# An mLSTM cell and a GELU layer: the layer's float32 block products replaced by three float32r products of 12-bit parts

## The chip, the cores and the metric

The kernel runs on one core of a Trainium2 chip. The metric is the device time of one execution in microseconds (us): 517.14 us is the median of three executions of the kernel before (516.58 to 518.07). The profile shows one execution, of 515.2 us from its first to its last instruction. PE is the matrix engine, PEld its weight loads, DVE the vector engine, ACT the scalar (activation) engine, POOL the general engine, SP the queue that issues most transfers.

## The reference, cut to what matters

```python
B, H, S, D = 4, 8, 768, 40          # q, k, v, o_gate: (B,H,S,D); i_gate, f_gate: (B,H,S)
for t in range(S):                   # the mLSTM cell, stabilised by a running maximum m
    m_new = maximum(f[t] + m, i[t])
    C = exp(f[t] + m - m_new) * C + exp(i[t] - m_new) * outer(v[t], k[t])
    n = exp(f[t] + m - m_new) * n + exp(i[t] - m_new) * k[t]
    y[t] = sigmoid(o[t]) * (C @ q[t]) / maximum(abs(n @ q[t]), 1)
    m = m_new
x = y as (3072 tokens, 320)
h = x @ w_in                         # (320, 2048)
out = (0.5 * h * (1 + erf(h / sqrt(2)))) @ w_out      # (2048, 320)
```

The weights arrive as float64; both kernels fetch their bits and convert them to float32 on chip. The sequence is cut into six chunks of 128 time steps. A chunk holds 512 tokens (four batches of 128 steps). Chunk 0 is handled in a front part, together with the conversion of the weights; "later chunks" are chunks 1 to 5. "The cell" of a chunk is its share of the mLSTM; "up" is `x @ w_in` and "down" is `gelu(h) @ w_out`.

## The kernel before: the parts that matter here

The later chunks compute up and down in float32 with a block scheme in which 7 products of half-size blocks take the place of 8 (sums of blocks of the weights, of x and of the hidden values are formed by DVE). Up works on two 128-row blocks of x (`NX = 2`), plus a rest of 64 rows that is done directly, with two halves side by side in the array.

```python
def product(to, lhs, rhs, f0, first, last):            # up: one block product, 2 tiles, moving 256 columns
    for j in range(2):
        nc.tensor.matmul(to[:, j, :], lhs[:, (f0 + j) * P:(f0 + j + 1) * P], rhs, ...)      # L597

def products(f0, to_sum):                              # seven of them for each pair of 128-wide tiles
    c11, c12, c21, c22 = [pool.tile([P, 2, HT], F32, name="pu", tag=tag)
                          for pool, tag in ((ps_tr, "tr"), (ps_h, "h"), (ps_mm, "a"), (ps_mm, "b"))]
    product(c11, a11, b11, f0, True, False)
    nc.scalar.copy(out=blk[1][1], in_=c11)
    product(c12, s2, t2, f0, True, True)
    nc.vector.tensor_tensor(out=blk[0][0], in0=c12, in1=blk[1][1], op=OP.add)
    ...                                                # c21, c22, then c11, c12, c21 again

def rest(f0, pair, h):
    for j in range(2):
        for e in range(2):
            nc.tensor.matmul(pair[e][:, j, :], w_rest[halves[e], ...], xT[halves[e], NX, ...], ...)   # L626
...
add_to = lambda blk, e, h, x, y: (
    nc.vector.tensor_tensor(out=blk[e][h], in0=x, in1=y, op=OP.add),                        # L639
    nc.scalar.activation(out=blk[e][h], in_=blk[e][h], func=AF.Gelu))                       # L640

# down: seven products, each in two steps t of 8 matmuls with 160 moving columns (HD = 160)
for j in range(HF):
    nc.tensor.matmul(bank[at][:, i, :], lhs(j, t), rhs(j), ...)                             # L682
return [lambda ...: product(...) for x in todo for t in range(2)]       # 14 steps, "F" in the order below

# a later chunk: all of up, then down interleaved with the cell of the next chunk
DOWN = """M0 Z M1 T0 W0 F F T1 W1 Z G3 Z F S0 Z S1 C0 M2 Z C1 G1 G0 M3 V0 Y0 Z V1 W2 Z F F T2 W3 F T3 F G2 Z
    Y1 S2 S3 C2 V2 C3 Y2 V3 F F Y3 X0 F F X1 X2 F F X3 F"""
```

The letters are steps of the next chunk's cell for batch 0 to 3: M masks on POOL, T transposes q and k (two PSUM banks, copied out by ACT), W eight exponentials on ACT, G a sigmoid on ACT, S scores (two banks, multiplied with W by DVE), C carries the state (one bank, read by three DVE operations), V values (one bank), Y the division on DVE and POOL, X transposes y to x (one bank). The banks for T and X come from a pool of two (`ps_tr`); S, C and V also use `ps_mm` and `ps_h`.

Of the kernel before, what the change touches and what calls it, by code (L numbers as in the profile page):

```python
# [9 lines left out]
F32 = mybir.dt.float32  # L10
BF16 = mybir.dt.bfloat16
# [6 lines left out]
I23 = 2.0 ** 23  # L18

# [8 lines left out]
    K K J T0 W0 O6 M2 O7 A J W1 S0 C0 K J T1 L7 U U K Z K V0 T2 A M3 J J G1 S1 K W2 W3 K C1 Z A S2 Z V1 G2 J Y0 J K  # L28
    C2 Z T3 J K Y1 U U J S3 Z V2 C3 K J K K J J F K F F F Z J K J X0 K K J F F F Z J F K G3 Y2 F J K V3 J K F K X1 J
    J F F F F K Z X2 B8 J F Y3 X3 B9 F"""  # L30
DOWN = """
    M0 Z M1 T0 W0 F F T1 W1 Z G3 Z F S0 Z S1 C0 M2 Z C1 G1 G0 M3 V0 Y0 Z V1 W2 Z F F T2 W3 F T3 F G2 Z Y1 S2 S3 C2
    V2 C3 Y2 V3 F F Y3 X0 F F X1 X2 F F X3 F"""
# [3 lines left out]
def kernel(  # L37
# [41 lines left out]
    outp = ctx.enter_context(tc.tile_pool(name="outp", bufs=2))  # L79
# [8 lines left out]

    w_in = const.tile([P, NX, 2, DFF // 2], F32, name="w_in")
    w_rest = const.tile([P, DFF // 2], F32, name="w_rest")
    w_out = const.tile([P, NF, DM], F32, name="w_out")
# [3 lines left out]
    xT = const.tile([P, NX + 1, TG], F32, name="xT")  # L98
# [31 lines left out]
    def load_M(n):  # L130

        if n >= NCH * B:
            return
        c, b = divmod(n, B)
        Mb[n] = wts.tile([P, H, L], F32, name="Mb", tag="Mb", bufs=NM)
        nc.sync.dma_start(out=Mb[n].rearrange("p h l -> p (h l)"),
                      in_=M_d[c - 1, b * H:(b + 1) * H, :].rearrange("h l -> (h l)").unsqueeze(0).to_broadcast([P, H * L]))
# [113 lines left out]
    for f in range(0, DFF // 2, WP // 2):  # L251
        for x in range(NX):
            pieces.append(([w_src["in"][x * P:(x + 1) * P, w_cols(e, f, WP // 2)] for e in range(2)],
                           w_in[:, x, :, f:f + WP // 2]))
        if f % WP == 0:
            pieces.append(([w_src["in"][NX * P:DM, w_cols(e, f, WP)] for e in range(2)], w_rest[:, f:f + WP]))
    n_in = len(pieces)
    for f in range(NF):
        pieces.append(([w_src["out"][f * P:(f + 1) * P, :]], w_out[:, f, :]))
# [32 lines left out]
    def conv_two(i):  # L292

        if i < len(pieces):
            hi, p = bits.pop(i)[:, :, 1], pow2.pop(i)
            pu = p.bitcast(U32)
            nc.vector.scalar_tensor_tensor(out=pu, in0=hi, scalar=0x80000000, in1=pu,
                                           op0=OP.bitwise_and, op1=OP.bitwise_or)
            dst, s = pieces[i][1], sig.pop(i)
            if len(dst.shape) == 3:  # L300
                s, p = [t.rearrange("p (e f) -> p e f", e=2) for t in (s, p)]
            nc.vector.scalar_tensor_tensor(out=dst, in0=s, scalar=2.0 ** -20, in1=p, op0=OP.mult, op1=OP.mult)
            fetch(i + NB)
# [18 lines left out]
    class Cell:  # L322
# [14 lines left out]
        def weights(self, b):  # L337

            n = self.c * B + b
            W[n] = wts.tile([P, H, L], F32, name="W", tag="W")  # L340
            if self.c > 0:
                M_n = Mb.pop(n)
# [37 lines left out]
        def weigh_values(self, b):  # L380
            vw = self.vw[b] = two.tile([P, H, D1], F32, name="vw", tag="vw")
# [3 lines left out]
        def scores(self, b):  # L385
# [3 lines left out]
            pool, tag = (ps_tr, "tr") if self.c > 0 and b % 2 else (ps_mm, "a")  # L389
# [10 lines left out]
        def carry(self, b):  # L400
# [4 lines left out]
            pf = ps_h.tile([P, H + NP, D1], F32, name="pf", tag="h")  # L405
# [10 lines left out]
            if c > 0:  # L416
# [4 lines left out]
                self.far[b] = two.tile([P, H, D1], F32, name="far", tag="far")  # L421
# [13 lines left out]
        def values(self, b):  # L435
# [3 lines left out]
            pool, tag = (ps_mm, "a") if self.c > 1 else (ps_h, "h")  # L439
# [9 lines left out]
            nc.vector.tensor_tensor(out=hs, in0=ph, in1=self.far.pop(b), op=OP.add)  # L449

# [11 lines left out]
        def turn_y(self, b):  # L462
# [8 lines left out]
            nc.scalar.copy(out=xT[:, :, t], in_=px)  # L471
            if self.c > 0:
                load(n + NLD)
            if self.c > 0 and b == B - 1:
                sum_x()


    HF, HT, HD = NF // 2, TG // 2, DM // 2

    Bm = [[lambda j, e=e, n=n: w_out[:, HF * e + j, HD * n:HD * (n + 1)] for n in range(2)] for e in range(2)]
    w_sums, in_sums, x_sums = [], [], []
    T = {1: lambda j: w_sums[0][:, j, :], 2: lambda j: w_sums[1][:, j, :], 3: Bm[0][1]}

    def sums_begin():

        gate_ctx.close()
        pool = ctx.enter_context(tc.tile_pool(name="sums_of", bufs=1))
        w_sums.extend(pool.tile([P, HF, HD], F32, name=f"w_sums{n}") for n in range(2))
        in_sums.extend(pool.tile([P, DFF // 2], F32, name=f"in_sums{n}") for n in range(3))
        x_sums.extend(pool.tile([P, HT], F32, name=f"x_sums{n}") for n in range(3))

    def weight_sum(n):
        x, y = {1: (Bm[0][1], Bm[0][0]), 2: (Bm[1][1], T[1]), 3: (Bm[1][1], Bm[0][1])}.get(n) or (Bm[1][0], T[2])  # L500
        if n == 4:

            parts = [raw.tile([P, 3, HD], F32, name="t4", tag=tag) for tag in ("sig", "pow", "sig")]
            T[4] = lambda j: parts[j // 3][:, j % 3, :]

        def step(j):
            nc.vector.tensor_tensor(out=T[n](j), in0=x(j), in1=y(j), op=OP.subtract)

        return [lambda j=j: (step(j), step(j + 1)) for j in range(0, HF, 2)]

    class Hidden:


        def __init__(self, summed):
            self.t = gp.tile([P, NF, TG], F32, name="g", tag="g")
            if summed:
                self.s1, self.s2 = [[raw.tile([P, HF // 2, HT], F32, name="sums", tag="bits", bufs=NB)
                                     for _ in range(2)] for _ in range(2)]

    def hidden_sums(g, f0, f1):  # L520

        (a11, a21), (_, a22) = [[g.t[:, HF * e + f0:HF * e + f1, HT * h:HT * (h + 1)] for h in range(2)]
                                for e in range(2)]
        s1, s2 = [t[f0 // (HF // 2)][:, f0 % (HF // 2):f0 % (HF // 2) + f1 - f0, :] for t in (g.s1, g.s2)]
        nc.vector.tensor_tensor(out=s1, in0=a21, in1=a22, op=OP.add)
        nc.vector.tensor_tensor(out=s2, in0=s1, in1=a11, op=OP.subtract)
        nc.vector.tensor_tensor(out=a21, in0=a11, in1=a21, op=OP.subtract)

    def up_step(g, sets):

        banks = []
        for k, (i0, i1, t0, t1) in sets:
            banks.append([ps_mm.tile([P, i1 - i0, t1 - t0], F32, name="pu", tag="ab"[k % 2]) for e in range(2)])
            for e in range(2):

                for i in range(i0, i1):
                    for x in range(NX):
                        nc.tensor.matmul(banks[-1][e][:, i - i0, :], w_in[:, x, e, i * P:(i + 1) * P], xT[:, x, t0:t1],  # L538
                                         start=(x == 0 and i == i0), stop=False, skip_group_check=True)
        for pu, (_, (i0, i1, t0, t1)) in zip(banks, sets):  # L540
            for i in range(i0, i1):
                for e in range(2):
                    r = halves[e]
                    nc.tensor.matmul(pu[e][:, i - i0, :], w_rest[r, i * P:(i + 1) * P], xT[r, NX, t0:t1], start=False,  # L544
                                     stop=(i + 1 == i1), skip_group_check=True)
        for pu, (_, (i0, i1, t0, t1)) in zip(banks, sets):
            for e in range(2):
                nc.scalar.activation(out=g.t[:, i0 + HF * e:i1 + HF * e, t0:t1], in_=pu[e], func=AF.Gelu)
# [12 lines left out]
    def first_up():  # L561
        if len(ups) == 1:
            tags_next.append(1)
        if ups:
            up_step(first_g, ups)
# [6 lines left out]
    def in_sum(i):  # L572
        f, (a11, a12), (a21, a22) = slice(WP * (i // 4), WP * (i // 4 + 1)), *[[w_in[:, x, e, :] for x in range(NX)]
                                                                               for e in range(2)]
        s1, s2, s4 = in_sums
        to, x, y, op = ((s1, a21, a22, OP.add), (s2, s1, a11, OP.subtract), (a21, a11, a21, OP.subtract),
                        (s4, a12, s2, OP.subtract))[i % 4]
        nc.vector.tensor_tensor(out=to[:, f], in0=x[:, f], in1=y[:, f], op=op)

    def x_blocks():  # L580
        return [[xT[:, x, HT * h:HT * (h + 1)] for h in range(2)] for x in range(NX)]

    def sum_x():
        (b11, b12), (b21, b22) = x_blocks()
        t1, t2, t4 = x_sums
        for to, x, y in ((t1, b12, b11), (t2, b22, t1), (b12, b22, b12), (t4, b21, t2)):
            nc.vector.tensor_tensor(out=to, in0=x, in1=y, op=OP.subtract)

    def summed_up(g, sums_too):
        (a11, s3), (a12, a22) = [[w_in[:, x, e, :] for e in range(2)] for x in range(NX)]  # L590
        s1, s2, s4 = in_sums
        (b11, t3), (b21, b22) = x_blocks()
        t1, t2, t4 = x_sums
        def product(to, lhs, rhs, f0, first, last):

            for j in range(2):
                nc.tensor.matmul(to[:, j, :], lhs[:, (f0 + j) * P:(f0 + j + 1) * P], rhs, start=(first and j == 0),  # L597
                                 stop=(last and j == 1), skip_group_check=True)

        def products(f0, to_sum):  # L600

            blk = [[g.t[:, HF * e + f0:HF * e + f0 + 2, HT * h:HT * (h + 1)] for h in range(2)] for e in range(2)]
# [196 lines left out]
```

## Time and profile before, and how to read them

| part of the 515.2 us | from, to (us) | length |
|---|---|---|
| front: chunk 0, gates, conversion of the weights, cell of chunk 1 | 0 to 133.19 | 133.2 |
| each of chunks 1 to 3: up, then down with the next chunk's cell | 133.19, 212.77, 292.35 | 79.6 each |
| chunk 4 | 371.93 | 77.7 |
| chunk 5 (no cell left) | 449.64 | 65.6 |

| engine | busy us | share of the span |
|---|---|---|
| PE | 500.3 | 97% |
| DVE | 340.2 | 66% |
| ACT | 255.0 | 49% |
| POOL | 60.9 | 12% |

Matmuls are pipelined, so the mean duration that a row prints is longer than the distance from one to the next. What a stream of matmuls costs is read from the chain of waits, which prints the length of a run of them together with their count. A float32 matmul of the source appears as two matmul records.

### The profile page before, as it was taken

The page shows a single profiled execution, that of the slowest core. Times are in us where ns is not written, and L with a number is a line of the kernel's source. Part 1 is how long each engine was busy: PE and PEld are TensorE (multiplying, and loading weights), DVE is VectorE, ACT ScalarE, POOL GpSimd, SP SyncE. Part 2 cuts the span into 40 slices and gives each one's busy share as a digit, 9 for nine tenths or more (in the row PEclk, how much of TensorE's full clock was granted, in tenths as well). Part 3 has the DMA queues.
Part 4 walks back from the last instruction along what each step waited for, and adds up shares of the span by engine and source line. Part 5 has one row for each costly group of instructions (what it writes and reads, how often), then busy time and mean ns, then how long its engine had stood idle before and what let it go on. Part 6 is the DMA issues. An engine that isn't in the chain of part 4 may idle for free.

```text
span 515.2 us, 10957 instructions
## 1 busy us (share of the span) xinstructions
PE 500.3 (97%) x4472; PEld 450.6 (87%) x4472; DVE 340.2 (66%) x696; ACT 255.0 (49%) x523; POOL 60.9 (12%) x98
## 2 busy tenths in 40 slices
PE   4889999999999999999999999999999999999997
PEld 3778888767888999988999988999988999988997
DVE  7789598999577887347668347678347657237621
ACT  7696999555344960152980132982123882124300
POOL 3002100000210225000145000053000021000000
PEclk9799999999999999999999999999999999999999
DMA  6999751279900254900234900124920020000001
GB/s 128 223 214 212 184 147 53 64 163 171 198 0 1 84 116 58 167 0 2 74 88 69 167 28 1 43 83 81 166 52 2 5 80 1 27 27 0 1 2 51
DMA packets 111442, 41.62 MB, mean 81 GB/s; under 512 B 101184, under 2 KB 104416, under 8 KB 111392
## 3 DMA queue, kind: packets, MB, share of 16 engines
q1 hardware_dynamic: 111392, 40.92, 37.5%
q8 instruction: 35, 0.57, 0.5%
q14 instruction: 15, 0.12, 0.1%
HBM read 36.90 MB, written 4.01 MB: 79 GB/s over the span
## 4 chain that ended last, share of the span: by engine, by line
PE 91%; ACT 4%; DVE 3%; issue 0%; DMA 0%; SPq 0%; DVEq 0%; ACTq 0%
PE po L682 30%; PE pu L597 24%; PE pu L626 7%; PE po L659 7%; PE pu L538 5%; PE ps L395 4%; PE ph L444 4%; PE pt L373 4%; PE pf L419 2%; PE pf L414 2%; PE pu L544 1%; PE px L470 1%; ACT W L359 1%; ACT pow L285 1%; ACT pow L286 1%; DVE M L194 1%
## 5 line engine op out<-in xcount | busy, mean ns | idle before, releaser
L682 PE MATMUL po<-w_out,g 128*128 128x160 f32 x640 | 91.5, 299 | 0.0
L682 PEld LDWEIGHTS po<-w_out,g 128*128 128x128 f32 x640 | 88.0, 190 | 0.3 <-DVE g L639 0.3
L597 PE MATMUL pu<-xT,w_in 128*128 128x256 f32 x240 | 58.8, 381 | 0.0
L639 DVE TENSOR_TENSOR g<-pu,g 128x512 f32<-128x512 f32 x60 | 40.5, 689 | 22.4 <-PE pu L626 21.0
L597 PEld LDWEIGHTS pu<-xT,w_in 128*128 128x128 f32 x240 | 45.0, 190 | 7.5 <-ACT g L640 1.7
L471 ACT COPY xT<-px 128x384 f32<-128x384 f32 x24 | 11.1, 480 | 77.9 <-PE px L470 77.8
L359 ACT ACTIVATE W<-Mb,aT 128x128 f32<-128x128 f32 x160 | 48.9, 391 | 0.1
L682 PE MATMUL po<-w_sums,sums 128*128 128x160 f32 x320 | 47.3, 302 | 0.0
L398 DVE TENSOR_TENSOR W<-ps,W 128x512 f32<-128x512 f32 x48 | 30.2, 683 | 23.9 <-PE ps L395 21.2
L334 POOL TENSOR_SCALAR_AFFINE_SELECT Mb<-Mb 128x1024 f32<-128x1024 f32 x20 | 22.9, 1155 | 185.3 <-DMA Mb<-M_d 131.2
L682 PEld LDWEIGHTS po<-w_sums,sums 128*128 128x128 f32 x320 | 44.0, 190 | 0.4
L606 ACT COPY g<-pu 128x512 f32<-128x512 f32 x20 | 11.6, 582 | 58.2 <-PE pu L597 58.2
L695 DVE TENSOR_TENSOR o_sb<-po,o_sb 128x320 f32<-128x320 f32 (+1 forms) x27 | 12.5, 463 | 39.4 <-PE po L682 36.2
L637 ACT ACTIVATE g<-pu 128x512 f32<-128x512 f32 x20 | 12.0, 598 | 52.7 <-PE pu L626 52.7
L597 PE MATMUL pu<-x_sums,in_sums 128*128 128x256 f32 x160 | 37.8, 379 | 0.0
L626 PE MATMUL pu<-xT,w_rest 64*128 64x256 f32 x320 | 37.2, 382 | 0.0
L640 ACT ACTIVATE g<-g 128x512 f32<-128x512 f32 x60 | 36.1, 627 | 1.9
L608 DVE TENSOR_TENSOR g<-pu,g 128x512 f32<-128x512 f32 x20 | 13.8, 692 | 34.6 <-PE pu L597 28.8
L626 PEld LDWEIGHTS pu<-xT,w_rest 64*128 64x128 f32 x320 | 30.1, 187 | 6.4 <-issue 3.3
L659 PE MATMUL po<-w_out,g 128*128 128x320 f32 x128 | 35.7, 434 | 0.0
L597 PEld LDWEIGHTS pu<-x_sums,in_sums 128*128 128x128 f32 x160 | 30.2, 190 | 4.3
L659 PEld LDWEIGHTS po<-w_out,g 128*128 128x128 f32 x128 | 23.8, 190 | 9.3
(140 smaller groups left out, 884.3 us busy)
## 6 DMA issues: line engine op xcount, KB each, us to landing
Mb<-M_d SPq DMA_DIRECT2D x20, 512.0 KB, 3.7
bits<-in_moe_w_in_dram SPq DMA_DIRECT2D x20, 256.0 KB, 4.6
bits<-in_moe_w_out_dram SPq DMA_DIRECT2D x16, 320.0 KB, 3.0
vb<-in_v_dram SPq DMA_DIRECT2D x24, 160.0 KB, 4.9
ob<-in_o_gate_dram SPq DMA_DIRECT2D x24, 160.0 KB, 4.2
qb<-in_q_dram SPq DMA_DIRECT2D x24, 160.0 KB, 4.0
kb<-in_k_dram SPq DMA_DIRECT2D x24, 160.0 KB, 4.5
out_dram<-o_sb SPq DMA_DIRECT2D x24, 160.0 KB, 3.0
```

Source lines behind the costliest of these rows:

```text
L334: nc.gpsimd.affine_select(out=t, in_=t, compare_op=OP.is_ge, fill=1.0e30, base=0, pattern=[[0, H], [1, L]], channel_multiplier=-1)
L359: nc.scalar.activation(out=W[n][:, h, :], in_=src, func=AF.Exp, scale=-1.0, bias=aT[:, self.c, r:r + 1])
L373: nc.tensor.transpose(pt[:, p, :], src[n % NLD][:, 2 * p:2 * p + 2, :].rearrange("p h d -> p (h d)"), ident)
L395: nc.tensor.matmul(ps[hip][:, p, :], kT[r, p, :], qT[r, p, :], start=True, stop=True)
L398: nc.vector.tensor_tensor(out=w, in0=ps[hip], in1=w, op=OP.mult)
L538: nc.tensor.matmul(banks[-1][e][:, i - i0, :], w_in[:, x, e, i * P:(i + 1) * P], xT[:, x, t0:t1], start=(x == 0 and i == i0), stop=False, ...
L597: nc.tensor.matmul(to[:, j, :], lhs[:, (f0 + j) * P:(f0 + j + 1) * P], rhs, start=(first and j == 0), stop=(last and j == 1), skip_group_c ...
L626: nc.tensor.matmul(pair[e][:, j, :], w_rest[halves[e], (f0 + j) * P:(f0 + j + 1) * P], xT[halves[e], NX, HT * h:HT * (h + 1)], start=False ...
L639: nc.vector.tensor_tensor(out=blk[e][h], in0=x, in1=y, op=OP.add),
L640: nc.scalar.activation(out=blk[e][h], in_=blk[e][h], func=AF.Gelu))
L659: nc.tensor.matmul(po[b], g.t[:, f, b * L:(b + 1) * L], w_out[:, f, :], start=(f == 0), stop=(f == NF - 1))
L682: nc.tensor.matmul(bank[at][:, i, :], lhs(j, t), rhs(j), start=(first and i == 0 and j == 0), stop=(i == n - 1 and j == HF - 1), skip_grou ...
```

## The change

In the later chunks every float32 operand is split into exact parts of few bits, and each float32 product becomes three products in the type float32r. With base 4097 a weight is w = 4097·w_hi + w_lo. For a moving (or hidden) value x there are x_hi (x rounded to few bits), x_all = x − x_hi, and x_lo = x_hi − x·4096/4097. Then w_hi·x_hi + w_lo·x_lo + (w_hi + w_lo)·x_all = w·x/4097, and the factor 4097 is put back by the `scale` of the activation that reads the result. There are no block products and no sums of blocks any more. What it is for: the same float32 result from fewer passes of the matrix engine.

```diff
+PART = 1.0 - 2.0 ** -13
+BASE = 1.0 + 2.0 ** -12
-DOWN = """ ... (above) """
+STEADY = """
+    U M0 M1 F T0 F W0
+    U S0 F C0 F T1 W1
+    U V0 S1 F C1 F M2 G0 G1 G2 G3
+    U V1 Y0 F T2 F W2 M3
+    U S2 Y1 F C2 F T3 W3
+    U V2 S3 F C3 F Y2
+    U V3 F Y3 F
+    U X0 X1 F X2 X3 F"""
...
+    def split_weight(w, hi, lo):
+        nc.scalar.activation(out=hi, in_=w, func=AF.Copy, scale=PART * 2.0 ** -12)
+        nc.vector.scalar_tensor_tensor(out=lo, in0=hi, scalar=-BASE * 2.0 ** 12, in1=w, op0=OP.mult, op1=OP.add)
+    def both(out, hi, lo):
+        nc.vector.tensor_tensor(out=out, in0=hi, in1=lo, op=OP.add)
...
+    def split(x, hi, all_, lo):
+        nc.scalar.activation(out=hi, in_=x, func=AF.Copy, scale=PART)
+        nc.vector.tensor_tensor(out=all_, in0=x, in1=hi, op=OP.subtract)
+        nc.vector.scalar_tensor_tensor(out=lo, in0=x, scalar=-1.0 / BASE, in1=hi, op0=OP.mult, op1=OP.add)
+    def split_x(px, t):          # after the transposes X; replaces one ACT copy and the sums of x
+        nc.scalar.activation(out=hi, in_=px, func=AF.Copy, scale=PART)
+        nc.vector.tensor_tensor(out=parts["x_all"][:, :, t], in0=px[:, 0:NX], in1=hi[:, 0:NX], op=OP.subtract)
+        nc.vector.tensor_tensor(out=parts["x_all_rest"][:, t], in0=px[:, NX], in1=hi[:, NX], op=OP.subtract)
+        nc.vector.scalar_tensor_tensor(out=parts["x_lo"][:, :, t], in0=px, ...)
...
+    class Stream:
+        def up(self):                                  # "U": one pair of 128-wide tiles, all 512 tokens
+            pu = [ps_h.tile([P, TG], F32, name="pu", tag="h") for e in range(2)]
+            w_parts = (parts["in"][i], in_lo[i], self.in_both[:, k % 2])
+            for e in range(2):
+                for n, (w, x) in enumerate(zip(w_parts, (x_hi, x_lo, x_all))):
+                    for j in range(NX):
+                        nc.tensor.matmul(pu[e], w[:, j, e, :], x[:, j, :], ...)
+            ...                                        # the rest: 3 x 2 matmuls of 64 rows, 512 columns
+            for e in range(2):
+                nc.scalar.activation(out=self.g[:, e], in_=pu[e], func=AF.Gelu, scale=4097.0)
+            if k + 1 < len(self.pairs):
+                self.make_in(k + 1)                    # one DVE add, 128x512
+        def finish_up(self, k, e):
+            if c == 1:
+                split_out(f)                           # w_out's tile is split once, in chunk 1
+            both(self.out_both[e], parts["out"][:, f, :], out_lo[f])
+            split(self.g[:, e], *[parts["g"][:, e, n, :] for n in range(3)])
+        def down(self):                                # "F": one 128-wide tile of the pair before
+            for n, b in order:                         # 3 parts x 4 batches
+                nc.tensor.matmul(self.po[b], parts["g"][:, e, n, b * L:(b + 1) * L], w_parts[n], ...)
+            ...                                        # then finish_up(k, e) for the pair last put up
...
     for c in range(1, NCH):
-        ...                                            # summed_up(g, ...), then DOWN
+        order = STEADY if c + 1 < NCH else "U F F " * HF + "F F"
+        if c == 1:                                     # no F in the first row, and "U Z" in the later rows
```

Z is now `split_in`, which splits one tile of w_in; four of the eight stand in the front and the rest in chunk 1. The weights are held tile by tile. From chunk 2 on, the cell's scores, carry and values take their PSUM banks from the same pool of two as its transposes (`ps_tr`), because up holds both banks of `ps_h` and down the four of `ps_mm`. The mask tile M is turned into W in place, `vw` and `far` have one buffer instead of two, and the loads of q, k and v for the next chunk are issued earlier (after V). Chunk 0 is computed in float32 as before.

## The prediction, made before the changed kernel had run

> **What bounds the kernel now.** I read the page's engine shares first, then the chain of waits in order of time, then the busy time by stretch, then the rows of the costliest groups. The engine shares and the slices:
>
> ```profile
> PE 500.3 (97%) x4472; PEld 450.6 (87%) x4472; DVE 340.2 (66%) x696; ACT 255.0 (49%) x523; POOL 60.9 (12%) x98
> PE   4889999999999999999999999999999999999997
> PEclk9799999999999999999999999999999999999999
> ```
>
> PE has no gap after the front and runs at full granted clock, so only PE time counts there. The chain of waits for chunk 2:
>
> ```profile
> 212.77 12.09 PE pu L597 x56
> 224.86 3.65 PE pu L626 x32
> 228.51 12.28 PE pu L597 x56
> 240.79 3.65 PE pu L626 x32
> 244.45 1.02 PE pt L373 x8
> 245.47 4.35 PE po L682 x32
> ...
> 252.87 1.99 PE ps L395 x32
> 254.85 0.60 PE pf L414 x16
> 255.45 0.59 PE pf L419 x16
> ```
>
> It is PE end to end. It also gives true spacings: an up record with 256 columns 12.09/56 = 216 ns, a down record with 160 columns 4.35/32 = 136 ns, a 64-row rest record 3.65/32 = 114 ns (two side by side), a transpose 0.87/8 = 109 ns. Chunk 5, which has no cell, gives down alone as 30.64 us for 224 records. Busy time of the up stretch and the down stretch of chunk 2 (length, PE, PEld, DVE, ACT, POOL, clock, DMA):
>
> ```profile
> 212.77:244.45 31.68, 31.68 (x177) 26.91 (x177) 18.69 (x29) 10.53 (x18) 0.00 (x0) 1.00 0.18 31
> 244.45:292.35 47.90, 47.90 (x589) 47.22 (x590) 30.77 (x60) 25.17 (x58) 14.44 (x20) 1.00 0.47 94
> ```
>
> The reader sees PE busy for all of both stretches, DVE for 49.5 of 79.6 us, ACT for 35.7. Up costs 31.7 us, down 30.6, and the cell what is left of 47.9, 17.3 us of PE. Those 62.3 us of up and down are what the change replaces, five times over.
>
> **What the Trainium skill says.** "FP8 and Floating Point Precision", section "TensorE Precision Notes": true float32 takes four passes of the array, reduced-precision float32 reads the four bytes and cuts them to FP22. The trace agrees on four passes: a source matmul is two records of 216 ns for 256 columns, 432 ns in all. No run so far shows a float32r matmul. "TensorE: Matmul & The Clock Gate", section "Back-to-back issue gap": about N/2.4 + 2.5 ns for one pass of N columns at full clock. A float32 record makes two passes, so 256 columns should take 2·256/2.4 + 2.5 = 215.8 ns against 216 measured, and 160 columns 135.8 against 136: the trace agrees. In the same page, section "LDWEIGHTS", a load of 128 columns takes 128/1.2 = 107 ns; the transposes' 109 ns would fit that bound, while the 136 ns stream hides it. "ScalarE: Activation LUTs", section "What ACT_TABLE_LOAD costs", speaks of some 2.7 us for a change of function set; the trace has 1283 ns, and I use that.
>
> **The change, part by part.** *Up.* Before: 31.7 us a chunk. After, for each of 8 pairs: 12 matmuls of 512 columns in one record and one pass. I choose 216 ns, the spacing of a 256-column two-pass record, which streams as many columns: 2.59 us. The 6 rest matmuls, side by side in pairs, at 114 ns: 0.68 us. Together 3.27 us, and 26.2 us a chunk.
>
> *Down.* Before: 30.6 us. After: 16 tiles × 12 matmuls of 320 columns. One pass of 320 is as long as two of 160, so 136 ns: 1.64 us a tile and 26.1 us a chunk. The weight load per record is the same 128 columns that now hides at this spacing.
>
> Up and down together 52.3 against 62.3 us: 10.0 us less a chunk, 50 us over five. This is the ratio of 3 one-pass products to 7/8 of four passes (3.5), diluted by the rest, which goes from four passes to three.
>
> *DVE.* Removed: the adds into g (four 128x512 at 0.69 us for the seven products of each pair, and more), the sums of hidden values, the output adds. Added, with durations of equal shapes from the rows:
>
> ```profile
> L639 DVE TENSOR_TENSOR g<-pu,g 128x512 f32<-128x512 f32 x60 | 40.5, 689 | 22.4 <-PE pu L626 21.0
> L302 DVE SCALAR_TENSOR_TENSOR w_out<-sig,pow 128x320 f32<-128x320 f32 x16 | 7.9, 492 | 0.6
> L398 DVE TENSOR_TENSOR W<-ps,W 128x512 f32<-128x512 f32 x48 | 30.2, 683 | 23.9 <-PE ps L395 21.2 <-ACT W L359 2.6
> ```
>
> A pair costs 0.69 for the sum of w_in's parts, and for each tile 0.49 (w_out's sum, 320 columns) + 0.69 + 0.69: 4.43 us, 35.4 a chunk. The cell keeps its own 19.0 us (8 × 0.683 scores, 4 × 0.49 far, 8 × 0.32 state, 4 × 0.50 values, 4 × 1.77 division). The split of x adds about 0.42 + 0.28 + 0.55 = 1.25 a batch, 5.0 a chunk. Sum 59.4 us, of a PE time of 52.3 + 17.3 = 69.6 us: 85% of it, where it was 62%. In chunk 1 the split of w_out (16 × 0.49) and of four tiles of w_in (4 × 0.69) come on top: 70 us.
>
> *ACT.* 16 Gelu (0.60) 9.6, 16 copies for g's high part (0.58) 9.3, 32 exponentials 9.8 (the timeline has eight in 2.45 us), sigmoids 1.9, copies of q, k, x and output 8.3. Gelu now alternates with exponentials in rows 1, 2, 4, 5 of the order and with the sigmoid in row 3: ten function-set loads of 1.28 us, 12.8. Sum 52 us of 69.6. Row 1 is the tight one: some 9.5 us of ACT beside 7.4 us of PE.
>
> *Waits that are new.* All of the cell's PSUM now comes from two banks, so C0 waits for DVE's multiplication of S0, the T after it for the reads of C, and those stand in DVE's queue behind the splits of g. At the chunk's end the next U needs x_lo and x_all of batch 3; DVE then has two splits of x and one of g to do (about 4.5 us) while PE has one down tile (1.6 us) and the x_hi products: I put 2.5 us there, and 1.5 us on the rest of the row order. That is 4 us a chunk for four chunks, 16 us, and 4 more in chunk 1, where DVE's 70 us exceed PE's. These 20 us are a judgement, not a sum.
>
> *Front and end.* The conversion has the same 26 pieces; eight sums of w_in leave (5.5 us of DVE), four splits of w_in with the two of the rest come, and the x split of chunk 1 lies at the end of the front: I add 1.5 us to 133.2. The tail after the last matmul stays at 515.2 − 512.0 = 3.3 us.
>
> *The sum.* 134.7 front + 5 × 52.3 = 261.5 + 4 × 17.3 = 69.2 + 20 waits + 3.3 tail = 488.7 us of span. The measured time was 1.9 us above the span: 490.6, say **490 us**, 5% less.
>
> **The rivals.** (1) *Everything hides*: the waits vanish because adjacent instructions on DVE and ACT overlap (four 0.683 us multiplications took 2.48 us in the timeline, eight exponentials of 0.39 us 2.45). Then about 470 us. For it: DVE and ACT stay under 90%, and the order staggers producers and consumers by half a row. Against: both queues are in order, and two banks carry six steps of the cell.
> (2) *DVE takes over as the bound*: with bank waits each row pays a DVE round trip. Rows with S, C and Y have 9 us of DVE beside 9.5 us of PE. At 80 us for each of chunks 1 to 4 only chunk 5 gains; 134.7 + 4 × 80 + 55.6 + 3.3 + 1.9 = 515 us, no change. For it: the 85%. Against: PE has slack of a whole U (3.3 us) between a split and its use.
> (3) *float32r is not what I take it for*. If it needs two passes, up and down double to 104.6 us a chunk, and the time is about 490 + 262 = 750 us. If the weight load shows beside 320 columns and the spacing is 165 instead of 136 ns, 5.6 us a chunk return and the time is 518 us. For it: no record here shows the type. Against: the change pairs it with widths 512 and 320 where one pass is longer than the 107 ns load, and it would have no purpose at two passes.
> (4) *The front grows*: pieces of w_in are fetched in four narrower transfers instead of two, and the x split comes on DVE where conversions pace the last down steps. DVE was busy 111.7 of 133.2 us there; I allow up to 5 us.
>
> **Range and chances.** The mechanism alone is worth 50 us; waits may eat from 0 (470) to nearly all (515). Most of the weight lies on 8 to 35 us of waits and front loss, so the range is 472 to 508. Faster by over 2% means below 506.8: I give 0.85. Within 2% 0.08 (rival 2, or a partly exposed weight load), slower 0.07 (rival 3, or rival 2 with a grown front).
>
> **What would show it.** In the profile after: up matmuls of 512 columns at 216 ns and down matmuls of 320 at 136 ns in chunk 5, which should last about 52 to 55 us plus the last tile's two down steps; one record per source matmul (192 down and 96 + 48 up records a chunk). Chunks 2 to 4 at 72 to 75 us, with PE's waits on DVE (x_lo, the cell's banks) and a dent at each chunk's end. DVE near 85% and ACT near 75% busy there. The prediction is wrong if chunk 5 is not near 54 us (then float32r's rate is the step that failed), or if chunk 5 is right and chunks 2 to 4 are far from 73 us (then the waits were misjudged), or if the front is far from 135 us.

## The result, and the profile after

The changed kernel takes 551.36 us (median of four, 550.62 to 552.15) against 517.61 us for the kernel before on the same chip: a ratio of 1.0657, 95% interval 1.0638 to 1.0675. It is slower by 6.6%. The profiled execution spans 550.4 us.

The engine shares and slices of the changed kernel's page:

```profile
PE 503.9 (92%) x4152; PEld 417.9 (76%) x4152; DVE 377.8 (69%) x802; ACT 330.6 (60%) x639; POOL 70.2 (13%) x98
PE   3989989997857989979999989999989999999997
PEclk9699999999978999999999999999999999999999
```

PE has dents in the front and in chunk 1 (slices 10 to 17) and small ones once a chunk after that; in chunk 1 its granted clock falls too. Busy PE is no lower than before. The same kernel's busy time by stretch, for chunks 1 to 5, cut at each chunk's first up matmul (length, PE, PEld, DVE, ACT, POOL, clock, DMA):

```profile
143.90:238.80 94.90, 80.40 (x679) 67.73 (x678) 65.51 (x126) 58.55 (x114) 19.41 (x22) 0.93 0.26 57
238.80:321.80 83.00, 79.56 (x702) 67.04 (x701) 57.32 (x116) 50.19 (x94) 17.53 (x20) 1.00 0.30 66
321.80:403.70 81.90, 79.57 (x702) 67.05 (x702) 55.71 (x113) 50.09 (x94) 16.39 (x19) 1.00 0.30 67
403.70:483.00 79.30, 77.44 (x639) 65.23 (x638) 49.80 (x105) 49.91 (x94) 5.58 (x6) 1.00 0.08 24
483.00:546.80 63.80, 63.05 (x362) 52.70 (x360) 34.34 (x62) 20.79 (x39) 0.00 (x0) 1.00 0.03 11
```

| part | before | predicted | after |
|---|---|---|---|
| front | 133.2 | 134.7 | 143.9 |
| chunk 1 | 79.6 | 77.6 less a pair's down (3.3) | 94.9 |
| chunks 2, 3, 4 | 79.6, 79.6, 77.7 | 73.6 each | 83.0, 81.9, 79.3 |
| chunk 5 | 62.3 | 52.3 and a pair's down | 63.8 |
| tail | 3.3 | 3.3 | 3.6 |

The last chunk has no cell, and PE never waits in it for long. Its chain of waits shows what a pair of tiles costs:

```profile
506.36 2.78 PE pu L643 x12
509.14 0.90 PE pu L649 x5
510.04 3.71 PE po L681 x24
513.74 2.78 PE pu L643 x12
```

A pair repeats after 7.38 us (506.36 to 513.74). Eight pairs are 59.1 us where 52.3 were predicted and 62.3 stood before: up and down gain 3.2 us a chunk, not 10.0. Chunks 1 to 4 take 22, 6.6, 5.5 and 4.8 us more than pairs plus cell (59.1 + 17.3, less 3.7 in chunk 1 and 1.9 in chunk 4, whose cell carries no state on). Together with 10.7 us in the front that outweighs the gain of 16.

My theories: (1) a float32r matmul takes longer than the one pass at bfloat16's rate that I had put for it; (2) waits that come from the order of the work on ACT and DVE make the dents; the rival throughout: ACT and DVE simply have too much to do.

### The profile page after: what moved, and what is told of

It reads as the page before. It is cut to its first block, busy times and chain, and to the rows that moved or that the text cites. A ratio compares the mean times of both kernels' runs of the same rounds, so it can differ in the third digit from the quotient of the medians.

```text
span 550.4 us, 10781 instructions
## 1 busy us (share of the span) xinstructions
PE 503.9 (92%) x4152; PEld 417.9 (76%) x4152; DVE 377.8 (69%) x802; ACT 330.6 (60%) x639; POOL 70.2 (13%) x98
## 4 chain that ended last, share of the span: by engine, by line
PE 64%; DVE 19%; ACT 12%; issue 4%; DMA 1%; SPq 0%; DVEq 0%; ACTq 0%
PE po L681 23%; PE pu L643 18%; PE pu L649 6%; PE ps L406 4%; PE pt L384 3%; ACT W L370 3%; PE ph L456 3%; PE pu L555 2%; PE pf L431 2%; ACT pow L300 2%; DVE x_lo L543 2%; PE pf L426 2%; DVE pow L312 1%; ACT pow L301 1%; DVE x_all L541 1%
## 5 line engine op out<-in xcount | busy, mean ns | idle before, releaser
L652 ACT ACTIVATE g<-pu 128x512 f32<-128x512 f32 x80 | 43.7, 595 | 86.7 <-PE pu L649 82.2
L530 ACT ACTIVATE parts_g<-g 128x512 fp32r<-128x512 f32 x80 | 50.6, 632 | 56.2 <-PE po L681 56.1
L681 PE MATMUL po<-parts_g 128*128 128x320 f32 x320 | 69.9, 333 | 0.0
L681 PE MATMUL po<-w_out,parts_g 128*128 128x320 f32 x320 | 62.9, 311 | 0.0
L681 PE MATMUL po<-out_both,parts_g 128*128 128x320 f32 x320 | 62.7, 310 | 0.0
L531 DVE TENSOR_TENSOR parts_g<-g,parts_g 128x512 fp32r<-128x512 f32 x80 | 58.0, 725 | 5.6 <-ACT parts_g L530 5.6
L532 DVE SCALAR_TENSOR_TENSOR parts_g<-g,parts_g 128x512 fp32r<-128x512 f32 x80 | 59.1, 739 | 0.0
L643 PE MATMUL pu<-x_lo,w_in 128*128 128x512 f32 x160 | 50.6, 397 | 3.6 <-DVE x_lo L543 3.6
L681 PEld LDWEIGHTS po<-w_out,parts_g 128*128 128x128 f32 x320 | 51.6, 189 | 0.0
L681 PEld LDWEIGHTS po<-out_both,parts_g 128*128 128x128 f32 x320 | 51.3, 190 | 0.0
L409 DVE TENSOR_TENSOR W<-ps,W 128x512 f32<-128x512 f32 x48 | 30.9, 685 | 29.5 <-PE ps L406 10.3
L643 PE MATMUL pu<-x_hi,w_in_hi 128*128 128x512 f32 x160 | 50.9, 400 | 0.0
L406 PE MATMUL ps<-qT,kT 64*128 64x128 f32 x384 | 32.4, 293 | 6.1 <-DVE hs L461 4.8
L406 PEld LDWEIGHTS ps<-qT,kT 64*128 64x128 f32 x384 | 28.1, 198 | 9.6 <-DVE hs L461 6.3
```

What stands on the lines that cost most here:

```text
L406: nc.tensor.matmul(ps[hip][:, p, :], kT[r, p, :], qT[r, p, :], start=True, stop=True)
L409: nc.vector.tensor_tensor(out=w, in0=ps[hip], in1=w, op=OP.mult)
L530: nc.scalar.activation(out=hi, in_=x, func=AF.Copy, scale=PART)
L531: nc.vector.tensor_tensor(out=all_, in0=x, in1=hi, op=OP.subtract)
L532: nc.vector.scalar_tensor_tensor(out=lo, in0=x, scalar=-1.0 / BASE, in1=hi, op0=OP.mult, op1=OP.add)
L643: nc.tensor.matmul(pu[e], w[:, j, e, :], x[:, j, :], start=(n == 0 and j == 0), stop=False, skip_group_check=True)
```

## The experiments

### What a float32r matmul costs alone

```diff
+ series("reduced512", wr, xr[:, 0:512]) ...   # 48 matmuls each, nothing else in the machine
+ series("bf512", wb, xb[:, 0:512]) ...
+ series("view512", top(wr), top(xr)) ...      # upper halves of the float32r tiles, read as bfloat16
```

> A kernel of its own that leaves out the whole computation: runs of 48 matmuls with nothing else in the machine, in float32 (160, 320, 512 columns), float32r (512 to 128 columns), bfloat16 (512, 320, 128), bfloat16 read as the upper halves of the float32r tiles, float32r with 64 and with 32 weight columns, and 64-row halves side by side. The trace of the changed kernel gives 233 ns for 512 float32r columns and 146 ns for 320, where 216 and 136 were predicted. Theory A (the type itself streams slower, in proportion to the columns, about 0.456 ns a column): 512 at 233, 384 at 175, 256 at 117, the same with 64 or 32 weight columns. Theory B (a fixed cost, an exposed weight load): 512 at 233, 384 at 180, 256 at 127, and back to 216 for 512 with 32 weight columns. Theory C (other engines disturb the reads in the kernel): 216 and 136 here. bfloat16: 216 and 136 in all theories.

One execution at a granted clock of 1.00. The chain of waits has the 48 float32r matmuls of 512 columns as one piece (start, length), which gives 10.92/48 = 227.5 ns:

```profile
107.23 10.92 PE reduced L43 x48
```

Rows of the other groups by shape (count, busy us and mean ns of one). Matmuls overlap, so the spacing is busy less one duration, over 47. (The row of the 512 columns, left out here, can't be read so: its first matmul starts while a float32 matmul is still running.)

```profile
L43 PE MATMUL reduced_w<-xr,wr 128*32 128x512 f32 x48 | 11.3, 394 | 0.0
L43 PE MATMUL view<-xr,wr 128*128 128x512 bf16 x48 | 11.0, 386 | 0.0
L43 PE MATMUL bf<-xb,wb 128*128 128x512 bf16 x48 | 10.5, 379 | 0.0
L43 PE MATMUL reduced<-xr,wr 128*128 128x320 f32 x48 | 7.2, 309 | 0.0
L43 PE MATMUL bf<-xb,wb 128*128 128x320 bf16 x48 | 6.7, 299 | 0.0
L43 PE MATMUL reduced<-xr,wr 128*128 128x256 f32 x48 | 5.9, 283 | 0.0
L43 PE MATMUL reduced<-xr,wr 128*128 128x128 f32 x48 | 5.5, 274 | 0.0
L43 PE MATMUL bf<-xb,wb 128*128 128x128 bf16 x48 | 2.8, 219 | 0.0
```

float32r takes 227.5 ns for 512 columns, 147 for 320 and 120 for 256; bfloat16 takes 216 and 136. From 256 to 512 columns float32r grows by 107.5 ns, 0.42 ns a column, and bfloat16 from 320 to 512 by 80 ns, 0.42 as well. So float32r does not stream slower; each matmul costs some 11 ns more, at 320 columns as at 512. Theory A, a time in proportion to the columns, fails: 256 columns take 120 ns, more than half of 227.5. Theory B is right to have a fixed cost (though 127 ns were expected for 256 columns), and wrong about its cause: with 32 weight columns instead of 128 the time does not fall (232 ns), so the length of the weight load is not what shows. The neighbours (C) are not needed for most of it, though in the kernel 512 columns take 232 ns (2.78/12 in the chain above), 4 more than here. What the 11 ns are stays open. At 128 columns float32r takes 111 ns and bfloat16 55: there the weight load would set the pace (the Trainium skill, "TensorE: Matmul & The Clock Gate", section "LDWEIGHTS", gives an estimate of 128 columns / 1.2 = 107 ns, and the run agrees within 4). bfloat16 read with a stride of four bytes takes 226 ns and, for 320 columns, 140: not the same as float32r, and not the same as packed bfloat16.

### The same inside the kernel

```diff
- nc.tensor.matmul(pu[e], w[:, j, e, :], x[:, j, :], ...)
+ nc.tensor.matmul(pu[e], top(w[:, j, e, :]), top(x[:, j, :]), ...)   # all float32r matmuls of the later chunks
```

> The changed kernel with every float32r matmul of the later chunks reading its operands as bfloat16 (the upper halves of the same tiles), so that ACT and DVE do exactly the same work and only the matrix engine's type differs; the low bits of the products are left out. If float32r's rate is what eats the gain (62.5 us for chunk 5 where 52.4 plus the last tiles were predicted), chunk 5 falls from 62.5 to about 56 us and each of chunks 2 to 4 by 4 to 6 us: about 525 us in all. If DVE and ACT set the pace of chunks 1 to 4, only chunk 5 falls: about 545 us.

539.3 us; chunks 1 to 5 took 94.4, 79.3, 79.7, 76.6 and 60.5. A pair of chunk 5 in this kernel's chain:

```profile
510.24 2.71 PE pu L647 x12
512.95 0.78 PE pu L653 x6
513.73 3.50 PE po L685 x24
```

That is 6.99 us against 2.78 + 0.90 + 3.71 = 7.39, eight times 0.40 us, and chunk 5 fell by 3.3 us. It was about half of what was expected, because the views do not stream at 216 and 136 either. Chunks 2 to 4 followed by 2.2 to 3.7 us, so PE sets most of their time. Chunk 1 fell by 0.5 only, which is within the 94.2 to 94.9 us of the runs that left it unchanged, so there PE's rate does not set the time.

### Changes between 128-row and 64-row matmuls

> A kernel of its own that leaves out the whole computation: the matrix engine's sequence of one pair of tiles, 16 times, with nothing else in the machine. (a) 12 float32r matmuls of 512 columns, 6 of 64 rows side by side, 24 of 320 columns, as the changed kernel has it; (b) the same without the 64-row ones; (c) with the 6 on all 128 rows; (d) as a, but with the 64-row ones of four pairs together. At the rates of the first run (233, 117, 146.5 ns) a should take 2.80 + 0.70 + 3.52 = 7.02 us a pair and b 6.31; the changed kernel takes 7.39 in chunk 5. Theory: each change between 128-row and 64-row matmuls costs about 0.19 us; then a 7.40, b 6.31, c 7.71, d 7.12. Rival: the 0.37 us in the kernel are waits for data or semaphores; then a 7.02 and d 7.02.

The chain of this kernel, a pair as in the changed kernel (a), then without the 64-row matmuls (b):

```profile
20.74 2.74 PE a_up L45 x12
23.49 0.90 PE a_up L51 x6
24.38 3.72 PE down L54 x24
28.10 2.75 PE a_up L45 x12
...
138.45 2.75 PE b_up L45 x12
141.19 3.52 PE down L54 x24
144.71 2.75 PE b_up L45 x12
```

A pair repeats after 7.36 us in a, as in the kernel, with no other engine at work. In b it is 6.26. The difference is 1.10 us, and the six 64-row matmuls alone cost 6 × 117 ns = 0.70; the other 0.40 us are the two changes, one before the rest (0.90 instead of 0.70) and one after it (3.72 instead of 3.52). With the rest on all rows (c) a pair takes 7.62, that is 6.26 and six full matmuls, with no change to pay for. With the rest of four pairs together (d) it takes 7.08 on average: two changes for four pairs, 0.23 us each by the same sum. So the longer float32r matmuls (12 × 16 ns and 24 × 10.5 ns, 0.44 us) and the two changes (0.40) account for a pair of 7.38 us where 6.54 were predicted; the kernel before changed four times a chunk for its rest, this one sixteen times.

```diff
-            for n, (w, x) in enumerate(((parts["rest"][u], parts["x_hi"][:, NX]), ...)):
-                ...                        # the rest's share of x @ w_in is left out
```

> The changed kernel without the 64-row rest matmuls of the later chunks (their share of x @ w_in is left out). If the rest costs its own 0.70 us a pair plus two changes of 0.19, a pair goes from 7.39 to 6.31 us, chunk 5 from 63.8 to about 55 us and each of chunks 2 to 4 by 7 to 9 us, total about 510 us. If the changes are free: 5.6 us a chunk, about 523 us. If DVE and ACT set the pace of chunks 1 to 4, only chunk 5 falls: about 542 us.

Chunk 5 went from 63.8 to 55.0 us, the pair in the chain to 2.78 + 3.50 = 6.28, as it should if each pair pays for two changes (without them chunk 5 would fall by 5.6 only). Chunks 2 to 4 fell by 5.8, 4.9 and 6.8, chunk 1 by 0.7: total 523.6 us. The total is the one expected if changes were free, but chunk 5, where nothing else is in the way, shows that they are not. In chunks 2 to 4 six of the eight rows of the order have a step of the cell on half the array (S or V) right behind the rest, so it shares the two changes and they stay when the rest goes. That leaves 8 × 0.70 + 2 × 0.40 = 6.4 us to gain (an estimate from the order and the costs above); PE's busy time in chunk 2 fell by 6.8 us, to 72.8.

### Chunk 1: the splits of w_in

In the changed kernel's chain, row 2 of chunk 1 (start, length; L652 is a function-set load and then Gelu, L504 the high part on ACT, L505 the low part on DVE, L409 the scores' product):

```profile
153.96 1.56 ACT W L370 x5
...
155.54 1.28 ACT L652
...
157.32 0.59 ACT g L652
157.92 0.53 ACT w_rest_hi L504
...
158.47 0.70 DVE w_rest L505
...
159.80 0.68 DVE w_in L505
160.49 0.61 DVE W L409
...
161.23 1.09 PE pf L426 x16
```

PE's carry (L426) waits for a bank that L409 frees; L409 stands behind the split in DVE's queue, the split behind Gelu on ACT, Gelu behind the exponentials.

```diff
- order = "U" + first + "U Z " + "U Z ".join(rest.split("U"))
+ rows = order.strip().split("\n"); each row + " Z"        # the split at the row's end
```

> The changed kernel with the four splits of w_in tiles in chunk 1 moved from just behind U to the end of their row. Theory: behind U they stand at the head of DVE's queue and wait for ACT (exponentials, two function-set loads and Gelu are ahead of them there), so that the multiplication of the scores and with it PE waits: chunk 1 falls from 96.4 to about 87 us, the total by 8 to 10 us. Rival: chunk 1 has too much ACT and DVE work for its PE time whatever the order (ACT 58, DVE 67 us): less than 3 us.

The splits that stood behind U in rows 2 to 5 now stand at the ends of rows 1 to 4, just ahead of that U. 544.9 us, 6.5 us less; chunk 1 took 87.4 instead of 94.9, the others were unchanged. This is most of the expected 8 to 10 us: the order cost 7.5 us, not the sum of the work, which was the same. The granted clock of chunk 1 rose with it from 0.93 to 0.98 and PE's busy time fell from 80.4 to 77.4 us, so of the 7.5 us 3.0 are less busy time of PE and 4.5 less idle time; no run separates the clock from the waits.

```diff
- nc.scalar.activation(out=self.g[:, e], in_=pu[e], func=AF.Gelu, scale=4097.0)
+ nc.scalar.activation(out=self.g[:, e], in_=pu[e], func=AF.Relu, scale=4097.0)   # GELU is left out
```

> The changed kernel with Relu in place of Gelu in the later chunks, so that the exponential's function set need not be changed for it: GELU is left out there, ACT's other work is the same. Theory: in chunk 1 PE waits for ACT (the chain runs through its set loads, Gelu, exponentials and splits), and the loads of 1.28 us are part of that: chunk 1 falls from 94.9 by 5 us or more, chunks 2 to 4 by 1 us or less each, since ACT has slack there. Rival: chunk 1 waits for DVE and the banks: less than 2 us.

542.0 us. The function-set loads fell from 21 + 19 + 9 (Gelu, exponential, sigmoid) to 8 and 9. Chunk 1 took 88.3 (6.6 less), chunks 2 to 4 81.3, 81.4 and 79.2 (1.7, 0.5, 0.1 less). So the set loads matter where PE waits for ACT's queue, in chunk 1, and hardly elsewhere. How the two edits overlap was not tried.

### The end of a chunk

The trace at 309 us has DVE's splits beside POOL's mask (timeline of the changed kernel):

```profile
309.36 2.90 POOL L347 TENSOR_SCALAR_AFFINE_SELECT W<-W 128x1024 f32<-128x1024 f32 x2
309.73 1.58 DVE L531 TENSOR_TENSOR parts_g<-g,parts_g 128x512 fp32r<-128x512 f32 x1
311.23 1.57 DVE L532 SCALAR_TENSOR_TENSOR parts_g<-g,parts_g 128x512 fp32r<-128x512 f32 x1
```

Each takes more than twice its usual 0.69 us. I took that for the cause of the wait at the chunk's end.

```diff
+            if self.c > 1:
+                return             # the mask of chunks 2 to 5 is left out
```

> The changed kernel with the causal mask (POOL's select over 128x1024) left out in chunks 2 to 5. Theory: the select doubles the time of DVE operations that run beside it (0.69 to 1.58 us in the trace at 309 us), and this is most of the 5 to 6 us that PE loses at each chunk's end: chunks 2 to 4 fall from 82 to 77 or 78 us, chunk 1 by as much, about 535 us in all. Rival: the two splits of x and the two banks of the transposes set that wait by themselves; then less than 1 us a chunk, 548 us or more.

548.9 us; chunks 1 to 5 took 93.7, 82.5, 81.9, 79.3 and 63.8. The splits that were slow now take 0.68 us (310.74 and 311.34 us in this kernel's timeline), and the chunks hardly change. The theory falls: slow as these operations were, PE was not waiting for them. In this kernel's chain the end of the chunk reads:

```profile
313.40 0.59 ACT g L654
314.00 0.39 ACT x_hi L542
...
314.41 0.42 DVE x_all L543
314.84 0.20 DVE x_all_rest L544
315.03 0.47 DVE x_lo L545
...
316.49 0.40 DVE out_both L510
316.89 0.60 DVE parts_g L533
```

x_hi waits for both Gelu on ACT, and a split of g stands between the splits of x on DVE. Two reorderings followed.

```diff
-    U X0 X1 F X2 X3 F
+    X0 X1 U f X2 X3 h F                    # f: down without its splits; h: those splits
```

> The changed kernel with only the last row of its order rewritten: the first two transposes of x come before U, and the third and fourth come before DVE's splits of g (row 8 becomes X0 X1, U, down without its splits, X2 X3, the splits, F). Theory: the 5 to 6 us that PE loses at the end of each of chunks 1 to 4 are one order of queues: x_hi stands behind two Gelu on ACT, and the split of batch 3 behind a split of g on DVE, while U waits for both. Then chunks 2 to 4 fall from 83.0, 81.9, 79.3 to about 78, 77 and 75 us and the total by 16 to 20 us. Rival: DVE simply has too much to do there (it is 70% busy over the chunk); then the wait moves to the next row and the total falls by less than 5 us.

570.8 us. This edit was a mistake: the splits of x now came before U in the order, so U used and waited for the next chunk's x (batches 0 and 1). It tests nothing of the theory. The same holds for the run that joined it with the next section's transfers and with the splits of w_in at the ends of rows 3 to 6.

> Both of these edits, and the splits of w_in in chunk 1 at the end of rows 3 to 6 (they stood behind U in rows 2 to 5; at the ends of rows 1 to 4 they gave 87.4 us for chunk 1). If the three causes add up: front 139, chunk 1 about 81, chunks 2 to 4 at 78, 77, 75, chunk 5 at 63.8 and 3.6 of tail: a span of 518 us, 519 in time, level with the kernel before. If they share one bottleneck (DVE and ACT): 530 us or more.

562.4 us, with chunks 2 to 4 at 88.4, 88.3 and 82.6.

```diff
-    U X0 X1 F X2 X3 F
+    x0 x1 U p0 p1 f x2 x3 p2 p3 h F        # x: transposes alone; p: the splits of x
```

> What the fifth run was meant to be: that one had the splits of the first two batches of x ahead of U, so that U used and waited for the next chunk's x. Here the last row is: transposes of two batches, U, their two splits, down without its splits, the other two transposes and splits, the splits of g, F; U reads the same x as in the changed kernel. Theory: the order of ACT's and DVE's queues makes the 5 to 6 us of waits at the chunk's end: chunks 2 to 4 from 83.0, 81.9, 79.3 to about 78, 77, 75, chunk 1 by 4 to 6 us, total 528 to 534 us. Rival: DVE's work sets it, less than 5 us in all.

548.0 us; chunks 2 to 4 at 81.6, 81.6 and 78.9. Only 1.4, 0.3 and 0.4 us less, far below the theory. U no longer waits for x, but the transposes of batch 3 wait for a bank until 317.4 us behind the same Gelu and splits, and the wait has mostly moved. What is left of chunks 2 to 4 is in good part not idle PE: of 83.0 us of chunk 2 PE is busy 79.6, 3 us more than 59.1 + 17.3. The changed kernel's chain shows where some of it goes (L384 transposes on the whole array, L406 works on 64 rows):

```profile
246.14 0.87 PE pt L384 x8
247.01 1.74 PE po L681 x12
...
252.40 0.89 PE ps L406 x16
253.29 1.95 PE po L681 x12
```

The same down tile takes 1.74 us behind the transposes and 1.95 behind the scores, and so throughout chunk 2: 0.2 us more, one change, wherever a step on half the array stands between two tiles. How much of the 3 us this makes was not tested.

### The front

> The changed kernel with each tile of w_in fetched in two transfers of 256 KB instead of four of 128 KB (20 transfers of w_in in all, as in the kernel before, instead of 32 and 4). Theory: the queue that issues transfers takes 0.43 us or more for each, the loads of k for chunk 1 come later by 5 us (the chain shows a wait of 4.5 us for one at 43 us), and this is about half of the 10.7 us by which the front grew: front from 143.9 to about 139 us. Rival: the front grew because splits of w_in and x share DVE and ACT with the conversion: front at 143 us or more.

The edit fetched both halves of a block of w_in in one transfer. 551.5 us, front 142.8 instead of 143.9. That is no gain: the front takes 142.0 to 144.1 us in the runs of other sections that leave it as it is. The number of transfers is not the cause.

```diff
- vw = ... tag="vw", bufs=1        + vw = ... tag="vw", bufs=2
- outp = ... bufs=B                + outp = ... bufs=3
```

> The changed kernel with two buffers for vw again, as the kernel before had (three output buffers in place of four make the room). Theory: with one buffer the weighting of v for the next batch, which stands in DVE's queue ahead of the matmul that frees the buffer, stops DVE in the front: the trace shows DVE idle for 4.2 us at 73.6 us and 1.8 us at 40.7 us until PE's carry matmuls, with the conversions of the weights behind it. Front from 143.9 to about 138 us, the rest unchanged: about 545.5 us. Rival: the front is set by the sum of its DVE and ACT work (splits of w_in and x), and the idle time is made good later: front at 142 us or more.

551.8 us, but the front took 138.7 instead of 143.9. DVE's timeline at that place in the changed kernel (the bracket is DVE's idle time before the operation and what ended it):

```profile
77.76 0.50 DVE L393 TENSOR_TENSOR vw<-vb,ewT 128x328 f32<-128x328 f32 x1 [4.18 <-PE pf L426]
```

And the timeline with two buffers:

```profile
71.60 0.49 DVE L393 TENSOR_TENSOR vw<-vb,ewT 128x328 f32<-128x328 f32 x1
```

With one buffer DVE idles 4.18 us until PE's carry, with the weight conversions behind it; with two it goes on. The front's gain came back as 0.3 to 1.5 us in each chunk and 0.9 in the tail.

> The changed kernel with three output buffers and nothing else. In the run with two vw buffers chunks 2 to 4 grew by 1.2 to 1.5 us each and the tail by 0.9 while the front shrank by 5.2. If the output buffers are the cause of the growth: front 143.9, chunks 2 to 4 at 84.4, 83.4, 80.5, tail 4.5, total 555 to 556 us, and the one vw buffer costs the front 5.2 us on its own. If the second vw buffer moved work from the front into the chunks: chunks as in the changed kernel, 551 us.

556.2 us: chunk 1 at 96.7, chunks 3 and 4 at 83.3 and 80.4, tail 4.4. Three output buffers alone cost 4.8 us (556.2 against 551.4), and beside them the second vw buffer saves 4.4 (551.8). Chunk 2 stayed at 83.0, against the expectation; the sum is right, its place not quite.

> The changed kernel with one step of the front moved: the transposes of batch 2 of chunk 1 (with the weighting of its v, which needs the one vw buffer) come after the carry of batch 1, which frees it, instead of before. Two vw buffers took the front from 143.9 to 138.7 us, but the three output buffers that made the room gave it back in later chunks. Theory: the order alone removes the stop of DVE, four output buffers stay: front about 139 to 140 us, the rest as in the changed kernel, total about 547 us. Rival: the later transposes delay the up steps and the scores of batch 2: front at 142 us or more.

Moving T2 behind C1 in the front's order gave 555.6 us and a front of 148.2: the rival. PE then waits for the transposes' copies (in the trace 4.5 us for qT).

Where the rest of the front's growth lies is in the chain of waits. Before, from 83.09 us to the front's end at 133.19, every piece is PE's, such as the first line here. In the changed kernel the pieces from 95.9 to 141.85 us are all DVE's and ACT's, and PE's last down steps come behind them (the other lines):

```profile
119.61 8.62 PE po L659 x32
...
138.33 0.34 DVE x_all L541
...
141.31 0.50 DVE w_out L315
...
141.85 2.42 PE po L601 x8
```

On that stretch the splits of w_in, of its rest and of x make 6.8 us, among the conversions of w_out. This is the second half of rival 4 in the prediction. No run moved these splits, so their share is read from the chain and not tested.

### Together

> The edits of the two runs before this one, and the splits of w_in in chunk 1 at the end of rows 3 to 6. If the causes add up: front 138, chunk 1 about 82, chunks 2 to 4 at 78, 77, 75, chunk 5 at 63.8, tail 3.6: span 517 us, time 519. If float32r's rate and the front's work leave more: 525 us. Either way what is left against the kernel before is the rate of float32r and the work of splitting.

Measured 539.9 us: front 138.4, chunk 1 85.8, chunks 2 to 4 83.1, 83.0 and 80.1, with three output buffers. That misses both expected sums by 15 us or more, most of it in chunks 2 to 4.

> The three changes of order together, with all buffers as in the changed kernel: the front's carry before the transposes, the splits of w_in at the ends of rows 3 to 6 of chunk 1, the splits of x ahead of the split of g. If they add up: front 139.5, chunk 1 about 85, chunks 2 to 4 at 81.6, 81.6, 78.9, chunk 5 62.7, tail 3.6: span 533, time 534 us. More than 540 us would mean that they take from each other.

Measured 542.3 us: front 145.3, chunk 1 84.3, then 81.6, 81.6, 78.9. Only the front missed its value (139.5): the move of T2 costs time there too.

> The two changes of order that helped, without the move in the front that cost 4 us: splits of w_in at the ends of rows 3 to 6 of chunk 1, and splits of x ahead of the split of g. Front 143, chunk 1 about 84.3, chunks 2 to 4 at 81.6, 81.6, 78.9, chunk 5 62.7, tail 3.6: span 536, time 537 us. This is the fastest form of the changed kernel that these experiments point to; it stays some 19 us above the kernel before.

Measured 537.8 us (ratio to the kernel before 1.0398, 1.0372 to 1.0424): front 142.0, chunk 1 84.8, then 81.6, 81.6, 79.0, 62.7. This is the lowest median of the forms that compute everything (its runs, 536.3 to 539.2, overlap those of the first form here, 537.7 to 541.9); it stays slower than the kernel before.

## Why the prediction was wrong

- **The passes: right.** One record per matmul, three products, no sums of blocks, and PE busy for 96% to 99% of chunks 2 to 5.
- **"I choose 216 ns ... one pass of 320 is as long as two of 160, so 136 ns": the term that was mis-sized.** float32r took 232 and 146.5 ns in the kernel. 96 × 16 + 192 × 10.5 ns = 3.6 us a chunk, 18 us in all. The rate per column was right (0.42 ns, as bfloat16); each matmul has some 11 ns on top, alone in the machine as well. Rival 3 named a longer spacing, but as an exposed weight load; the run with 32 weight columns speaks against that for these widths. The cause of the 11 ns stays open.
- **"The 6 rest matmuls ... at 114 ns: 0.68 us": mis-sized.** The matmuls are right (117 ns), two changes of row grouping per pair were not in the sum: 0.40 × 8 = 3.2 us a chunk, 16 us in all. The kernel before shows them (12.28 us after a rest against 12.09 for 56 records), and I read over it. The prediction's own sign, that a chunk 5 far from 54 us would mean float32r's rate, holds for half of the miss only. Both terms together make 34 of the 61.7 us by which the predicted span (488.7) was too low; corrected for them alone it would have been 523 us, already above the 515.2 of the kernel before.
- **"These 20 us are a judgement": they were 39.** The sums of work behind them were right (chunk 2: DVE 57.3 and ACT 50.2 us, against 59.4 and 52), so work alone, rival 2, was not the bound, although chunks 2 to 4 came near its 80 us: PE is busy for 79.6 us of chunk 2. Chunks 2 to 4 have 16.9 us beyond pairs and cell instead of 12, but that this is near is luck: only 7.6 of them are idle time of PE, and the other 9.3 are busy time that the sum lacked (in part the changes between cell steps and tiles). Of the waits, the chunk's end was named rightly as a place, but the order of the splits there explains only a small part of them (0.3 to 1.4 us a chunk in the run with x split first). Chunk 1 had 22 instead of 8 (14.5 of them idle time of PE, the rest busy time, with the granted clock at 0.93): I had summed DVE's work there and not read the order, in which a split on ACT and DVE stands ahead of the product that frees PE's bank. Moving it gave 7.5 us, no set loads 6.6.
- **"I add 1.5 us to 133.2": it was 10.7.** I listed vw's single buffer in the change and did not ask who waits for it in the front; that is 4 to 5 us. Of rival 4 the transfers are not the cause. For the other 5 to 6 us the chain points to its second half, the splits among DVE's conversions: I had counted DVE's work in the front and not seen that the front's path would change from PE to DVE and ACT. That part is not tested.
- **Chances.** The gain left to lose was 50 us in my sum and 16 in fact, so the 20 us of waits that I had allowed for were enough to turn the sign. The waits beyond them (19 us) and the front (9 us) made a small loss into 6.6%.

## What to carry to other kernels

Measure the rate of a data type that the trace does not hold before a sum is built on it: 11 to 16 ns on each matmul were a third of this change's expected gain. Measure it at several widths, too: one width can't tell a slower rate from a fixed cost. When work is cut into finer steps, count how often the matrix engine changes between full and half rows. When a buffer goes from two to one, or a step moves in the order, ask in every part of the kernel what stands behind it in the queue of the engine that will wait.

## What the runs showed of the hardware that I had not expected

- float32r: 120, 147 and 227.5 ns for 256, 320 and 512 columns, bfloat16 136 and 216 for 320 and 512: 0.42 ns a column for both, and some 11 ns more for each float32r matmul; at 128 columns 111 against 55 ns.
- bfloat16 read from every second position: 226 ns for 512 columns and 140 for 320, where packed it takes 216 and 136.
- A change from 128-row to 64-row float32r matmuls or back: about 0.20 us each (1.10 us a pair less 0.70 for six matmuls, two changes).
- A DVE operation of 0.69 us took 1.58 us beside a select of POOL over 128x1024; without the select it took 0.68 us.
